# Dividing softmax weights before the transposes: sums, splits and a later place for decoding

## The chip, the cores and the metric

The kernel runs on one core of a Trainium2 chip. The metric is device time in microseconds (us), the median of several executions. The engines are named as in the profile: PE is TensorE (PEld its weight loads), DVE is VectorE, ACT is ScalarE, POOL is GpSimd, SP issues DMAs. SBUF is the on-chip memory, PSUM the accumulator memory that PE writes.

## The reference, cut to what matters

Attention over q, k, v of shape (8, 8, 576, 64) keeps for each query the 32 largest scores, takes a softmax over them and multiplies by v. The result, 4608 tokens of width 512, goes through a layer without nonlinearity but a product:

```python
scores = scale * np.matmul(q, k.transpose(0, 1, 3, 2))
kth = np.partition(scores, -top_k, axis=-1)[..., -top_k:-top_k + 1]
scores = np.where(scores >= kth, scores, -1000000000.0)
attn = np.exp(scores - np.max(scores, axis=-1, keepdims=True))
attn = attn / (np.sum(attn, axis=-1, keepdims=True) + 1e-09)
x = np.matmul(attn, v)          # heads side by side: 4608 x 512
out = ((x @ w1) * (x @ w2)) @ w3 @ w_out
```

## The kernel before

Attention is cut into 144 slots. A *wide* slot is 128 queries of two heads (128 of them), an *ends* slot is the last 64 queries of four heads (16, two in each of the 8 batches). Twelve slots make 384 tokens, a block, and each of the 12 blocks is one pass through the layer (`moe_steps`): 192 matmuls into tiles `ab`, whose two halves are multiplied (ACT copies one half into `asb`, DVE multiplies, ACT and POOL write the high and low parts `g`), then 96 matmuls into `eo`. The kernel multiplies every operand as a high part and a low part, three products each: `x` has both, and so have `wh`/`wl`, `wf` and `g`.

The order on each engine is the order of the code (`InOrder`). The loop over p is a pipeline: iteration p takes the scores of slot p+1 (`scores`, PE into `st`, `take_scores`, ACT into `s`), picks the largest 32 of slot p (`top32_steps`, DVE), masks and exponentiates slot p-1 (`mask`, ACT and POOL; `exps`, ACT with a sum into `sums`), and turns slot p-2 and multiplies it by v. In between stand three calls of `fill`, each of 8 matmuls of the layer (`SHARE`), which also issue what the last finished product put off (`evict`), and seven *places* for start-up work (`warm`): at a place, each unit of weights under way takes one step. A unit loads 512 KB (`fetch`), is decoded from 64-bit storage (`decode`: ACT into `t` and `z`, then DVE, then POOL) and used: `load_w12` splits it, `load_w3` folds it on PE into `pf` (w3 and w_out are multiplied into one weight, `wf`). Forty units fill the first dozen slots; a new one starts at every second place.

For slot m = p-2 the order is: `invert` (POOL adds 1e-9 to the sums, DVE takes reciprocals), `spread` (POOL copies a wide slot's two reciprocals over 128 columns, tile `wide`), `turn` (PE transposes the weights `pab` into `tp` and `ro`, and `wide` into a further part of `ro`), `take_turned` (ACT copies `tp` into `pts` and `ro` into `pr`), `values` (PE multiplies by v, into columns 256 to 384 of `ro`; for an ends slot it also spreads the reciprocals with 8 small matmuls, which ACT copies), `normalise` (DVE multiplies the product by the turned reciprocals, in place in `pr`), `split_high` (ACT writes the high part of x from `pr`) and, in the next iteration, `split_low` (POOL subtracts to get the low part). `ro` has one buffer, `tp` and `st` share two.

Of the kernel before, what the change touches and what calls it, by code (L numbers as in the profile page):

```python
# [68 lines left out]
def attn_moe(ctx: ExitStack, tc: tile.TileContext, q, k, v, w1, w2, w3, w_out, out, flag, general):  # L69
# [44 lines left out]
    def decode(z, dst=None):  # L114
        t = ps_e.tile([128, CHUNK], F32, tag="t", name="t")
        high = z[:, 1 : 2 * CHUNK : 2]
        low = z[:, : 2 * CHUNK].bitcast(U16)[:, 1 : 4 * CHUNK : 4]
        r, u = z[:, 0 : 2 * CHUNK : 2].bitcast(I32), z[:, 2 * CHUNK :].bitcast(I32)
        act.activation(t, high, AF.Copy, scale=2.0**-112)
        act.activation(r, low, AF.Copy, scale=2.0**-13)  # L120
        yield
        ti = t.bitcast(I32)
        dve.tensor_scalar(u, ti, -(2**31), None, op0=ALU.bitwise_and)
        dve.scalar_tensor_tensor(u, ti, 3, u, op0=ALU.logical_shift_left, op1=ALU.bitwise_or)
        yield
        dst = z[:, 2 * CHUNK :] if dst is None else dst
        pool.tensor_tensor(dst.bitcast(I32), u, r, op=ALU.add)
        yield
        yield
        return dst  # L130
# [137 lines left out]
        pool.tensor_scalar(sums, sums, 1e-9, None, op0=ALU.add)  # L268
        dve.reciprocal(sums, sums)

    def spread(sums, hps):
        if len(hps) == 2:
            return None
        wide = att_p.tile([128, 128], F32, tag="wide", name="wide", bufs=1)
        pool.tensor_copy(wide[:].rearrange("p (a d) -> p a d", a=2), sums[:].unsqueeze(2).to_broadcast([128, 2, D]))
        return wide

    def turn(pab, wide):
        tp = ps_a.tile([128, 2, 512], F32, tag="a", name="tp")
        flat = pab[:].rearrange("p a c -> p (a c)")  # L280
        for a in range(2):
            for c in range(4):
                o = a * (S + 64) + c * 128
                pe.transpose(tp[:, a, c * 128 : (c + 1) * 128], flat[:, o : o + 128], ident)
        ro = ps_v.tile([128, 512], F32, tag="v", name="ro")
        pe.transpose(ro[:, :128], flat[:, 512:640], ident)
        if wide is not None:
            pe.transpose(ro[:, 128:256], wide, ident)
        return tp, ro

    def take_turned(tp, ro, wide):
        pts = att_p.tile([128, 2, 512], F32, tag="pts", name="pts", bufs=1)
        act.copy(pts, tp)
        pr = att_p.tile([128, 256], F32, tag="pr", name="pr", bufs=1)
        n = 128 if wide is None else 256
        act.copy(pr[:, :n], ro[:, :n])
        return pts, pr[:, :128], pr[:, 128:]

    def values(vts, hps, pts, pr, rec, sums, ro):
        rb, ov = ro[:, 128:256], ro[:, 256:384]  # L300
        ends = len(hps) == 2
        for i, h in enumerate(HEADS):
            if ends:
                for j in range(2):
                    pe.matmul(
                        rb[h, j * 64 : j * 64 + 64], sums[:, j : j + 1].to_broadcast([128, 64]), ident[:, HEADS[i ^ j]],
                        start=True, stop=True,
                    )
        for j, hp in enumerate(hps):
            vt = vts[hp]  # L310
            for c in range(5):
                for i, h in enumerate(HEADS):
                    block = i * 4 + c if c < 4 else (((8, 10), (10, 9))[j][i] if ends else 8 + i)
                    n = HEADS[i ^ j] if ends else slice(0, 128)
                    rhs = pr[:, n] if c == 4 else pts[:, j if ends else i, c * 128 + n.start : c * 128 + n.stop]
                    to = ov[h, j * 64 : j * 64 + 64] if ends else ov[h]
                    pe.matmul(to, vt[:, block * D : (block + 1) * D], rhs, start=(c == 0), stop=(c == 4))
        if ends:
            act.copy(rec, rb)
        return ov  # L320

    def width(t):
# [1 line left out]

    def new_x(n):
        return x_p[n % 2].tile([128, 2, NB], F32R, tag="x", name="x")

    def normalise(ov, rec):
        dve.tensor_tensor(rec, ov, rec, op=ALU.mult)

    def parts_of(tiles, lo, t, whole):
        n = width(t)
        return [(x[:, 0, lo : lo + n], x[:, 1, lo : lo + n], whole[:, j * n : j * n + n]) for j, x in enumerate(tiles)]
# [2 lines left out]
        act.copy(high, whole)  # L336

    def split_low(high, low, whole):
        pool.tensor_tensor(low, whole, high.bitcast(F32), op=ALU.subtract)

    def moe_steps(xs, nb, places, after):
        def take_a(p, asb):
# [46 lines left out]
    if general:  # L389
        outs = out.rearrange("e (b t) -> b e t", b=B)  # L390
        for src, step in startup:
            for _ in step(fetch(src)):
                pass
        settle()
        with tc.For_i(0, B, 1) as b:
            seen = small.tile([1, 1], I32, tag="seen", name="seen", bufs=1)
            nc.sync.dma_start(seen, flag[ds(b + 1, 1), :])
            with tc.If(nc.values_load(seen, min_val=0, max_val=1) > 0):
                kts = {hp: load_k(b, hp) for hp in range(NHP)}
                vts = {hp: load_v(b, hp) for hp in range(NHP)}  # L400
                for first, ts in ((0, range(3)), (NB, range(3, TAIL + 1))):
                    xs, lo = [new_x(0) for _ in range(NHP)], 0
                    for t in ts:
                        qt = load_q(b, t)
                        for hps in [hps for hps, u in slots_of(0) if u == t]:
                            s, st = new_s(), scores(qt, kts, hps)
                            for h in range(2):
                                take_scores(s, st, h)
                            edge = top32_exact(s)
                            pab, sums = new_weights()  # L410
                            for a in range(2):
                                mask(s, edge, pab, a)
                                exps(edge, pab, sums, a)
                            invert(sums)
                            wide = spread(sums, hps)
                            tp, ro = turn(pab, wide)
                            pts, pr, rec = take_turned(tp, ro, wide)
                            ov = values(vts, hps, pts, pr, rec, sums, ro)
                            normalise(ov, rec)
                            for part in parts_of([xs[hp] for hp in hps], lo, t, rec):  # L420
                                split_high(*part)
                                split_low(*part)
                        lo += width(t)
                    place = lambda es: outs[ds(b, 1)][:, es, first : first + lo].rearrange("o p n -> (o p) n")
                    for _ in moe_steps(xs, lo, [(place, slice(0, lo))], lambda f: f()):
                        pass
        return
# [72 lines left out]
    def warm():  # L500
        entered.append(p)
        if p < 0:
            return
        if fetched and len(entered) % 2 == 0:
            z, step = fetched.pop(0)
            going.append(step(z))
        going[:] = [unit for unit in going if next(unit, "end") != "end"]
        prefetch(WAITING)
# [9 lines left out]
    for p in range(-1, n_slots + 3):  # L518
        i, j, m = p + 1, p - 1, p - 2
        finder = top32_steps(ss[p], p) if 0 <= p < n_slots else iter(())  # L520
        if 0 <= m < n_slots:
            invert(pabs[m][1])
        folded = next(finder, None)
        warm()
        if 0 <= j < n_slots:
            edges[j] = edges_of(j)
        for part in fresh:
            split_low(*part)
        fresh.clear()
        if 0 <= m < n_slots:  # L530
            wide = spread(pabs[m][1], slots[m][1])
        if 0 <= j < n_slots:
            pabs[j] = new_weights()
            for a in range(2):
# [3 lines left out]
        begin()  # L538
        next(finder, None)
        if 0 <= m < n_slots:  # L540
            tp, ro = turn(pabs[m][0], wide)
            pts, pr, rec = take_turned(tp, ro, wide)
        if 0 <= j < n_slots:
            exps(edges[j], *pabs[j], 0)
        warm()
# [14 lines left out]
                renew_q(group_of[i] + 2)  # L560
        if 0 <= m < n_slots:
            b, hps, t = slots[m]
            ov = values(of(vts, b), hps, pts, pr, rec, pabs[m][1], ro)
            renew(vts, load_v, m)
        next(finder, None)
        warm()
# [3 lines left out]
        if 0 <= m < n_slots:  # L570
            n = m // BLOCK
            for hp in hps:
                if (n, hp) not in xs:
                    xs[n, hp] = new_x(n)
            normalise(ov, rec)
            fresh += parts_of([xs[n, hp] for hp in hps], column[group_of[m]], t, rec)
            for part in fresh:
                split_high(*part)
            del ss[m], pabs[m], edges[m]
            if (m + 1) % BLOCK == 0:  # L580
                starting.append(n)
# [67 lines left out]
```

## Time and profile before

| what | value |
|---|---|
| time of three runs | 1297.02 us median, 1296.96 to 1297.53 |
| the profiled execution's own time | 1297.56 us |
| its span | 1295.8 us |
| busy PE / PEld / DVE / ACT / POOL | 1225.3 / 1044.9 / 1178.8 / 954.4 / 840.7 us |
| granted TensorE clock, mean over the span | 0.973 |

The profiled execution runs from its first instruction to its last in 1295.8 us; 1.8 us lie around that. Busy time is the time in which an engine has an instruction under way; a busy PE counts matmuls that overlap each other, so its weight loads (PEld) are shown beside it. The run has three stretches: the start-up with the decoding of weights, up to about 193 us; the steady slots, up to about 1225 us; and the last block, which PE does alone.

### The profile page before, as it was taken

How to read it: one execution, taken by the hardware profiler on the slowest of the kernel's cores; microseconds unless marked ns; L12 is line 12 of the kernel's file. 1: busy time of each engine (PE TensorE's matmuls, PEld its weight loads, DVE VectorE, ACT ScalarE, POOL GpSimd, SP SyncE). 2: the span in 40 equal slices, each digit the busy share in tenths (PEclk: the TensorE clock that was granted, in tenths of full speed). 3: DMA queues.
4: the chain of work that ended last, by engine and by line, in shares of the span. 5: the costliest groups of instructions: out<-in, count | busy, mean ns of one | idle time of the engine just before them, and what ended most of it. 6: DMA issues, size and time to landing. Idle time of an engine off the chain costs nothing.

```text
span 1295.8 us, 27725 instructions
## 1 busy us (share of the span) xinstructions
PE 1225.3 (95%) x9617; PEld 1044.9 (81%) x9617; DVE 1178.8 (91%) x3932; ACT 954.4 (74%) x1961; POOL 840.7 (65%) x1169
## 2 busy tenths in 40 slices
PE   3788769999999999999999999999999999999996
PEld 1444448888888888888888888888888888888996
DVE  7899999999999999999999999999999999999610
ACT  5677777777777778777777778777777778777621
POOL 4777887757757757657657666767667666667520
PEclk7799969999999999999999999999999999999999
DMA  7334402110220012100210012000210011000000
GB/s 279 106 122 131 128 19 76 37 34 9 61 67 9 10 34 81 38 28 19 65 53 10 16 48 83 16 28 20 68 50 10 22 62 63 22 22 2 19 8 28
DMA packets 30122, 64.79 MB, mean 50 GB/s; under 512 B 5396, under 2 KB 11540, under 8 KB 29972
## 3 DMA queue, kind: packets, MB, share of 16 engines
q1 hardware_dynamic: 29972, 62.93, 14.8%
q8 instruction: 77, 1.26, 0.4%
q14 instruction: 73, 0.60, 0.1%
HBM read 53.48 MB, written 9.44 MB: 49 GB/s over the span
## 4 chain that ended last, share of the span: by engine, by line
PE 89%; DVE 5%; ACT 3%; POOL 2%; issue 1%; DMA 0%; SPq 0%; POOLq 0%; DVEq 0%; ACTq 0%
PE ab L58 33%; PE eo L58 16%; PE ro L58 16%; PE st L58 12%; PE tp L58 9%; PE pf L58 3%; DVE w L58 2%; DVE z L58 2%; POOL z L58 1%; DVE top L58 1%; ACT pab L58 1%; ACT z L58 0%; ACT s L58 0%; POOL wl L58 0%; ACT t L58 0%
## 5 line engine op out<-in xcount | busy, mean ns | idle before, releaser
L58 POOL TENSOR_TENSOR pab<-s,pab 128x576 f32<-128x576 f32 x288 | 404.1, 1425 | 127.2 <-DVE w L58 109.8
L58 DVE MAX8 top<-w 128x8 f32<-128x192 f32 (+1 forms) x1152 | 467.1, 447 | 0.0
L58 PE MATMUL ab<-x,wh 128*128 128x384 f32 x1536 | 403.6, 344 | 0.0
L58 ACT COPY pts<-tp 128x1024 f32<-128x1024 f32 x144 | 146.1, 1015 | 196.7 <-PE tp L58 196.7
L58 DVE MATCH_REPLACE8 w<-top,w 128x192 f32<-128x192 f32 x864 | 289.2, 342 | 0.0
L58 PEld LDWEIGHTS ab<-x,wh 128*128 128x128 f32 x1536 | 275.3, 189 | 0.0
L58 PE MATMUL ab<-x,wl 128*128 128x384 f32 x768 | 269.5, 351 | 0.0
L58 ACT ACTIVATE pab<-pab,edge 128x576 f32<-128x576 f32 x288 | 226.8, 788 | 0.9 <-POOL pab L58 0.9
L58 PE MATMUL eo<-g,wf 128*128 128x384 f32 x1152 | 225.8, 346 | 0.0
L58 ACT ACTIVATE pab<-s,edge 128x576 f32<-128x576 f32 x288 | 207.5, 768 | 15.6 <-POOL edge L58 15.6
L58 PEld LDWEIGHTS eo<-g,wf 128*128 128x128 f32 x1152 | 198.6, 188 | 7.5 <-issue 7.5
L58 ACT COPY s<-st 128x576 f32<-128x576 f32 x288 | 184.5, 641 | 18.8 <-PE st L58 18.8
L58 PE MATMUL st<-kt,qt 64*128 64x288 f32 (+1 forms) x1280 | 186.4, 439 | 12.5 <-DMA kt<-in_k 7.7
L58 DVE TENSOR_TENSOR w<-w,s 128x384 f32<-128x384 f32 x288 | 183.4, 637 | 4.9
L58 DVE TENSOR_TENSOR w<-s 128x384 f32<-128x384 f32 x288 | 168.1, 624 | 8.1 <-ACT s L58 7.6
L58 PEld LDWEIGHTS ro<-pts,vt 128*64 128x64 f32 x2560 | 129.2, 138 | 50.6 <-ACT g L58 28.3
L58 PE MATMUL ro<-pts,vt 128*64 128x128 f32 (+1 forms) x2560 | 162.3, 270 | 0.0
L58 PE MATMUL tp<-ident,pab 128*128 128x128 f32 x1152 | 151.7, 275 | 11.1 <-POOL wo L58 9.7
L58 PEld LDWEIGHTS st<-kt,qt 64*128 64x128 f32 (+1 forms) x1280 | 99.6, 181 | 74.5 <-ACT pr L58 30.4
L58 PEld LDWEIGHTS ab<-x,wl 128*128 128x128 f32 x768 | 144.3, 188 | 13.4 <-issue 12.3
L58 PEld LDWEIGHTS tp<-ident,pab 128*128 128x128 f32 x1152 | 136.1, 142 | 21.3 <-POOL wo L58 10.2
L58 POOL TENSOR_TENSOR g<-asb,g 128x384 fp32r<-128x384 f32 x96 | 96.8, 1009 | 86.4 <-ACT g L58 86.4
(51 smaller groups left out, 1259.8 us busy)
## 6 DMA issues: line engine op xcount, KB each, us to landing
z<-in_w SPq DMA_DIRECT2D x32, 512.0 KB, 3.6
vt<-in_v SPq DMA_DIRECT2D x32, 352.0 KB, 3.4
qt<-in_q SPq DMA_DIRECT2D x40, 256.0 KB, 2.7
kt<-in_k SPq DMA_DIRECT2D x32, 320.0 KB, 3.0
out_t<-osb SPq DMA_DIRECT2D x32, 192.0 KB, 1.9
z<-in_wo SPq DMA_DIRECT2D x8, 512.0 KB, 6.4
out_t<-osb SPq DMA_DIRECT2D x16, 160.0 KB, 1.8
out_t<-osb SPq DMA_DIRECT2D x16, 32.0 KB, 1.6
```

Of the source, the lines that this page charges most:

```text
L58: ins = fn(*args, **kw)
```

## The change

The weights of a slot are divided by their sums on ACT before they are transposed: `normalise` now takes the reciprocals as a scale for each partition and rewrites both halves of `pab`, two instructions of 128x576. `spread`, the tile `wide`, its transpose, the 8 small matmuls of an ends slot and ACT's copy of them go. The product by v is then x itself: `split_high` reads it from the bank `ro`, and `split_low`, which also reads that bank, moves from POOL to DVE, ahead of a place. `decode` yields once more, so everything after a unit's decoding happens a place later.

```diff
@@ decode
         pool.tensor_tensor(dst.bitcast(I32), u, r, op=ALU.add)
+        yield
         yield
         yield
@@
-    def spread(sums, hps):
...
-    def turn(pab, wide):
+    def normalise(pab, rec):
+        for a in range(2):
+            act.activation(pab[:, a, :], pab[:, a, :], AF.Copy, scale=rec[:, a : a + 1])
+
+    def turn(pab):
...
-        if wide is not None:
-            pe.transpose(ro[:, 128:256], wide, ident)
...
-        pr = att_p.tile([128, 256], F32, tag="pr", name="pr", bufs=1)
-        n = 128 if wide is None else 256
-        act.copy(pr[:, :n], ro[:, :n])
+        pr = att_p.tile([128, 128], F32, tag="pr", name="pr", bufs=1)
+        act.copy(pr, ro[:, :128])
...
-        for i, h in enumerate(HEADS):
-            if ends:
-                for j in range(2):
-                    pe.matmul(
-                        rb[h, j * 64 : j * 64 + 64], sums[:, j : j + 1].to_broadcast([128, 64]), ident[:, HEADS[i ^ j]],
-                        start=True, stop=True,
-                    )
...
-        if ends:
-            act.copy(rec, rb)
...
-    def normalise(ov, rec):
-        dve.tensor_tensor(rec, ov, rec, op=ALU.mult)
...
-        pool.tensor_tensor(low, whole, high.bitcast(F32), op=ALU.subtract)
+        dve.tensor_tensor(low, whole, high.bitcast(F32), op=ALU.subtract)
@@ the loop over p
         folded = next(finder, None)
+        for part in fresh:
+            split_low(*part)
+        fresh.clear()
         warm()
         if 0 <= j < n_slots:
             edges[j] = edges_of(j)
-        for part in fresh:
-            split_low(*part)
-        fresh.clear()
         if 0 <= m < n_slots:
-            wide = spread(pabs[m][1], slots[m][1])
+            normalise(*pabs[m])
...
-            normalise(ov, rec)
-            fresh += parts_of([xs[n, hp] for hp in hps], column[group_of[m]], t, rec)
+            fresh += parts_of([xs[n, hp] for hp in hps], column[group_of[m]], t, ov)
```

ACT, one steady slot in which `ab` products are put away; `x` is the high part, `pab<-s,edge` the mask, `pab,sums<-pab,edge` the exponential. Before:

```order
L58 COPY s<-st 128x2x288
L58 CAST x<-pr 128x128
L58 ACTIVATE pab<-s,edge 128x576 x2
L58 COPY asb<-ab 128x384
L58 COPY pts<-tp 128x1024
L58 COPY pr<-ro 128x256
L58 ACTIVATE pab,sums<-pab,edge 128x576
```

and after:

```order
L58 COPY s<-st 128x2x288
L58 CAST x<-ro 128x128
L58 ACTIVATE pab<-pab,sums 128x576 x2
L58 ACTIVATE pab<-s,edge 128x576 x2
L58 COPY asb<-ab 128x384
L58 COPY pts<-tp 128x1024
L58 COPY pr<-ro 128x128
L58 ACTIVATE pab,sums<-pab,edge 128x576
```

The two divisions stand between x and the next slot's masks, ahead of `asb` and `pts`; the copy into `pr` is half as wide.

DVE, from the last search of one slot into the next. Before:

```order
L58 MAX top_96<-w 128x8 x2
L58 TENSOR_TENSOR pr<-ro,pr 128x128
L58 RECIPROCAL sums<-sums 128x2
L58 TENSOR_TENSOR w<-s 128x2x192 x2
L58 TENSOR_TENSOR w<-w,s 128x2x192 x2
L58 MAX top_97<-w 128x8 x2
```

and after:

```order
L58 MAX top_96<-w 128x8 x2
L58 RECIPROCAL sums<-sums 128x2
L58 TENSOR_TENSOR w<-s 128x2x192 x2
L58 TENSOR_TENSOR w<-w,s 128x2x192 x2
L58 TENSOR_TENSOR x<-ro,x 128x128
L58 MAX top_97<-w 128x8 x2
```

The multiplication ahead of the reciprocal is gone, and the subtraction stands behind the four folding steps.

PE in the start-up, from the product by v to the next slot's; `pf` is the fold of w3. Before:

```order
L58 MATMUL ro<-pr,vt 64x128 x2
L58 MATMUL pf_953<-wo,z 128x512 x6
L58 MATMUL tp<-ident,pab 128x128 x8
L58 MATMUL ro<-ident,pab 128x128
L58 MATMUL ro<-ident,wide 128x128
L58 MATMUL pf_1062<-wo,z 128x512 x2
L58 MATMUL st<-kt,qt 128x288 x4
```

and after:

```order
L58 MATMUL ro<-pr,vt 64x128 x2
L58 MATMUL pf_1077<-wo,z 128x512 x8
L58 MATMUL tp<-ident,pab 128x128 x8
L58 MATMUL ro<-ident,pab 128x128
L58 MATMUL st<-kt,qt 128x288 x4
```

The two fold matmuls between the transposes and the scores now stand with the six behind the product by v.

## Rows read from the trace of the kernel before

**Rows 1.** The page: the chain that ended last, by engine.

```profile
PE 89%; DVE 5%; ACT 3%; POOL 2%; issue 1%; DMA 0%; SPq 0%; POOLq 0%; DVEq 0%; ACTq 0%
```

**Rows 2.** Stretches: length, busy us of each engine (instructions), clock, DMA share, GB/s.

```profile
core 0: us, PE busy (x) PEld busy (x) DVE busy (x) ACT busy (x) POOL busy (x), PEclk, DMA share, GB/s
28.59:192.68 164.09, 124.89 (x623) 69.72 (x624) 150.10 (x416) 122.58 (x234) 126.92 (x143) 0.84 0.32 102
...
431.39:439.29 7.90, 7.90 (x64) 6.97 (x63) 7.87 (x28) 6.30 (x13) 6.07 (x9) 1.00 0.00 0
455.16:463.10 7.94, 7.94 (x64) 7.00 (x63) 7.56 (x28) 5.91 (x12) 4.40 (x8) 1.00 0.08 27
```

**Rows 3.** The chain in order of time, one steady slot: start, us, work.

```profile
446.90 3.02 PE eo L58 x16
449.92 0.87 PE tp L58 x8
450.80 0.22 PE ro L58 x2
451.02 1.41 PE eo L58 x8
452.42 1.17 PE st L58 x8
453.59 1.24 PE ro L58 x20
```

**Rows 4.** Timeline of PE's loads, one steady slot; idle before and releaser bracketed.

```profile
460.29 0.79 PEld L58 LDWEIGHTS st<-kt,qt 64*128 64x128 f32 x8 [0.25 <-ACT pr L58]
461.46 0.85 PEld L58 LDWEIGHTS ro<-pts,vt 128*64 128x64 f32 x16 [0.38 <-ACT osb L58]
...
462.70 1.36 PEld L58 LDWEIGHTS eo<-g,wf 128*128 128x128 f32 x8 [0.17 <-issue]
```

**Rows 5.** The same in an ends slot, where the sums are spread.

```profile
516.93 0.32 PEld L58 LDWEIGHTS ro<-ident,sums 128*64 128x64 f32 x8 [0.39 <-ACT g L58]
517.16 0.56 PEld L58 LDWEIGHTS ro<-pts,vt 128*64 128x64 f32 x16
```

**Rows 6.** Timeline of ACT, the slot from 431.39 us.

```profile
431.71 1.44 ACT L58 ACTIVATE pab<-s,edge 128x576 f32<-128x576 f32 x2
433.06 0.46 ACT L58 COPY asb<-ab 128x384 f32<-128x384 f32 x1
434.97 1.01 ACT L58 COPY pts<-tp 128x1024 f32<-128x1024 f32 x1 [1.46 <-PE tp L58]
435.88 0.38 ACT L58 COPY pr<-ro 128x256 f32<-128x256 f32 x1
```

**Rows 7.** Timeline of DVE and POOL, the same slot.

```profile
431.46 1.00 DVE L58 TENSOR_TENSOR w<-s 128x384 f32<-128x384 f32 x2
432.01 0.78 POOL L58 TENSOR_TENSOR x<-pr,x 128x128 fp32r<-128x128 f32 x1
432.38 1.41 DVE L58 TENSOR_TENSOR w<-w,s 128x384 f32<-128x384 f32 x2
433.71 0.61 DVE L58 MAX8 top<-w 128x8 f32<-128x192 f32 x2
433.94 2.81 POOL L58 TENSOR_TENSOR pab<-s,pab 128x576 f32<-128x576 f32 x2 [0.59 <-DVE w L58]
434.89 0.55 DVE L58 TENSOR_TENSOR asb<-ab,asb 128x384 f32<-128x384 f32 x1
...
439.09 0.29 DVE L58 TENSOR_TENSOR pr<-ro,pr 128x128 f32<-128x128 f32 x1
439.29 0.15 DVE L58 RECIPROCAL sums<-sums 128x2 f32<-128x2 f32 x1
```

**Rows 8.** The chain in order of time, a slot of the start-up.

```profile
104.83 5.36 PE pf L58 x12
...
110.21 0.59 ACT wf L58
```

More of the change, by code (lines that the diff above doesn't have):

```diff
@@ L269, in invert @@
         dve.reciprocal(sums, sums)
-    def spread(sums, hps):
[L272 to L276, printed above, removed]
-    def turn(pab, wide):
+    def normalise(pab, rec):
+        for a in range(2):
+            act.activation(pab[:, a, :], pab[:, a, :], AF.Copy, scale=rec[:, a : a + 1])
+    def turn(pab):
         tp = ps_a.tile([128, 2, 512], F32, tag="a", name="tp")
@@ L286, in turn, with take_turned, values @@
         pe.transpose(ro[:, :128], flat[:, 512:640], ident)
-        if wide is not None:
-            pe.transpose(ro[:, 128:256], wide, ident)
         return tp, ro
-    def take_turned(tp, ro, wide):
+    def take_turned(tp, ro):
         pts = att_p.tile([128, 2, 512], F32, tag="pts", name="pts", bufs=1)
         act.copy(pts, tp)
-        pr = att_p.tile([128, 256], F32, tag="pr", name="pr", bufs=1)
-        n = 128 if wide is None else 256
-        act.copy(pr[:, :n], ro[:, :n])
-        return pts, pr[:, :128], pr[:, 128:]
-    def values(vts, hps, pts, pr, rec, sums, ro):
-        rb, ov = ro[:, 128:256], ro[:, 256:384]
-        ends = len(hps) == 2
-        for i, h in enumerate(HEADS):
-            if ends:
-                for j in range(2):
-                    pe.matmul(
-                        rb[h, j * 64 : j * 64 + 64], sums[:, j : j + 1].to_broadcast([128, 64]), ident[:, HEADS[i ^ j]],
-                        start=True, stop=True,
-                    )
+        pr = att_p.tile([128, 128], F32, tag="pr", name="pr", bufs=1)
+        act.copy(pr, ro[:, :128])
+        return pts, pr
+    def values(vts, hps, pts, pr, ro):
+        ov = ro[:, 256:384]
+        ends = len(hps) == 2
         for j, hp in enumerate(hps):
@@ L414, in attn_moe @@
                             invert(sums)
[L415 to L418, printed above, removed]
-                            normalise(ov, rec)
-                            for part in parts_of([xs[hp] for hp in hps], lo, t, rec):
+                            normalise(pab, sums)
+                            tp, ro = turn(pab)
+                            pts, pr = take_turned(tp, ro)
+                            ov = values(vts, hps, pts, pr, ro)
+                            for part in parts_of([xs[hp] for hp in hps], lo, t, ov):
                                 split_high(*part)
@@ L540, in attn_moe @@
         if 0 <= m < n_slots:
-            tp, ro = turn(pabs[m][0], wide)
-            pts, pr, rec = take_turned(tp, ro, wide)
+            tp, ro = turn(pabs[m][0])
+            pts, pr = take_turned(tp, ro)
         if 0 <= j < n_slots:
@@ L562, in attn_moe @@
             b, hps, t = slots[m]
-            ov = values(of(vts, b), hps, pts, pr, rec, pabs[m][1], ro)
+            ov = values(of(vts, b), hps, pts, pr, ro)
             renew(vts, load_v, m)
@@ L574, in attn_moe @@
                     xs[n, hp] = new_x(n)
-            normalise(ov, rec)
-            fresh += parts_of([xs[n, hp] for hp in hps], column[group_of[m]], t, rec)
+            fresh += parts_of([xs[n, hp] for hp in hps], column[group_of[m]], t, ov)
             for part in fresh:
```

## The prediction

> **What bounds the kernel now.** I read the chain that ended last first, then the stretches, then single slots. The chain is PE for 89% of the span [rows 1]. In order of time a steady slot is a closed row of PE work: 3.02 us (16 matmuls of the layer), 0.87 (eight transposes), 0.22 (two more, the second that of `wide`), 1.41 (8 matmuls), 1.17 (scores), 1.24 (product by v), in all 7.93 us [rows 3]. Two slots side by side say the same: one that puts `ab` products away has DVE busy 7.87 of 7.90 us, one in the `eo` part has DVE busy 7.56 of 7.94, and both take as long [rows 2]. An engine that set the time could not do 0.31 us less in the second without the slot getting shorter, so DVE, though nearly full, is not what the steady slots wait for. PE is. In a slot of the `ab` part ACT is busy 6.30 us and stands idle 1.46 in one piece ahead of `pts`, for the transposes [rows 2, 6].
>
> PE's loads leave 0.25 + 0.38 + 0.17 us between them in such a slot [rows 4]. The profile names ACT for two of these gaps and nothing for the third, but an ends slot has 0.39 us at the same place [rows 5], with other work on ACT; I read them as the price of going to another shape of matmul and back, and leave them in the sum.
>
> The start-up is another matter. From 28.59 to 192.68 us 13 slots take 164.1 us, 12.6 each, with DVE busy 150.1 us of it and PE 124.9 [rows 2]. Its chain goes through PE's folds, 5.36 us in one piece, and on to ACT's copy of the folded weight [rows 8]. The last stretch is PE alone on the last block; the change leaves it as it is.
>
> **The change part by part.** Steady slots first, PE. A wide slot loses the transpose of `wide`: two transposes take 0.22 us of the chain, so one is 0.11 [rows 3]. An ends slot loses 8 loads and matmuls that take 517.16 - 516.93 = 0.23 us from start to start [rows 5]; the gap of 0.39 in front of them stays, for the product by v follows. About 131 slots have their PE part behind 193 us, 16 of them ends slots: 115 x 0.11 + 16 x 0.23 = 12.7 + 3.7 = 16.3 us, all of it on the chain, if no other engine steps in. The new slot is 7.82 us.
>
> ACT. Two divisions of 128x576 from SBUF to SBUF with one operand for each partition are added. The trace has no such copy; the nearest row is the mask, an instruction of the same shape with one such operand, two of which take 433.06 - 431.71 = 1.35 us from start to start [rows 6]. Low end: 0, if ACT's idle time hides it all (less than that it cannot be, for instructions are added and none goes that is as long); high end: 1.8 to 2.0, twice the pace of the 128x1024 copy (435.88 - 434.97 = 0.91) or its duration of 1.01 [rows 6]. I take 1.35, since the shape is the same. The copy into `pr` halves from 256 columns; against `asb` (384 columns, 0.46 us; 256 take 0.38) 128 columns are worth some 0.1 us [rows 6], an estimate. `split_high` costs what it did. So an `ab` slot has 6.30 + 1.35 - 0.1 = 7.55 us of ACT in 7.82, an `eo` slot 5.91 + 1.25 = 7.16. What hides it is the idle 1.46 us ahead of `pts`; of that 1.46 - 1.25 - 0.11 = 0.1 is left, and a little more where x waited for DVE. Behind the divisions in ACT's queue stand the masks, `asb` and `pts`: if the cover is gone, `pts` is late, then the product by v, and each 0.1 us costs 131 x 0.1 = 13 us.
>
> The divisions wait for DVE's reciprocal, which no longer stands behind the multiplication; the transposes come 16 layer matmuls (3.02 us) behind the product by v, and the divisions need 1.35 of that plus x, so PE should not wait for them.
>
> DVE. It loses the multiplication (0.20 us, 439.29 - 439.09) and gets the subtraction, of the same shape and with one operand in PSUM as well: 0.20, or 0.29 at its full duration [rows 7]. The first pair of folding steps takes 432.38 - 431.46 = 0.92 us and the second 433.71 - 432.38 = 1.33 while POOL reads SBUF for x [rows 7]. POOL's x and `wide` go, so the second pair should come down to 0.92: 0.41 saved, 7.87 to 7.46. POOL only gains; its next mask waits for the folding [rows 7], which ends earlier. None of this is on the chain of the steady slots; it is worth nothing there. `ro` has one buffer and is now held until the subtraction, but PE writes it again only behind 16 layer matmuls and the transposes, some 3.9 us after the product; folding and subtraction need 1.84 + 0.2 from the reciprocal on.
>
> Start-up. DVE saves the same 0.41 us in 13 slots, 5.3 us, and here DVE is the fullest. It is idle 164.1 - 150.1 = 14.0 us. The later place takes away part of that: eight fold matmuls now stand in one piece behind the product by v, with their input decoded a place earlier, and ACT's copy of the folded weight no longer stands ahead of `pts`. At best all 14.0 go, 19.3 in all; at worst none of it, and ACT's 13 x 1.25 = 16.3 us fall on the chain instead: +16.3 - 5.3 = 11 us lost. ACT is busy 122.6 of 164.1 and goes to 139, still below DVE's 145. I take half of the idle time: 7.0 + 5.3 = 12.3 us.
>
> The sum: 1297.56 - 16.3 - 12.3 = 1269 us against the profiled execution, which lies 0.5 us above the median of the runs, within what they differ.
>
> **The rivals.** First, *ACT and DVE close a loop.* `asb` now stands behind the divisions, and DVE's product of the halves waits for it. From that product to the next reciprocal DVE takes 439.29 - 434.89 - 0.20 = 4.20 us [rows 7]; then come the reciprocal (0.08 from start to start), divisions 1.35, masks 1.35, `asb` 0.46 [rows 6], and two hand-overs of 0.15, as from DVE's folding (432.38 + 1.41 = 433.79) to POOL's mask at 433.94 [rows 7]: 7.74 us. That is below 7.82 by 0.08, so it is no luxury. If it comes out at 7.9 or more, the 86 slots of the `ab` part keep their old length and the gain is that of the `eo` and ends slots (some 8 us) and 4 to 9 us of the start-up: 1281 to 1286, up to 1291 if the start-up gives nothing.
>
> Second, the slow side: *the divided copy costs what the 1024-wide one does*, 0.91 to 1.01 us each. It decides from the point where the pair exceeds 7.93 - 6.20 = 1.73 us in an `ab` slot. At 1.82 to 2.02, ACT needs 8.02 to 8.22; 86 slots lose up to 0.29 us, 25 us, the `eo` slots (5.91 - 0.1 + 2.02 = 7.83) still gain 4, and the start-up gives about nothing: 1305 to 1318. For it speaks only that no such copy stands in the trace; against it the mask's row.
>
> Third, *nothing to be measured*: the start-up's chain does run through ACT in places [rows 8], and 13 x 1.35 = 17.5 us there would cancel the 16.3 of PE: about 1299.
>
> Fourth, *PE has room.* If the gaps of [rows 4] are waits for ACT that go, PE needs only 7.00 - 0.11 = 6.89 us and ACT and DVE set the slots: 7.55 in 8 of 12, 7.16 in 4, on average 7.42, so 131 x 0.51 = 67 us and the start-up's 12.3 go: 1218. The equal gaps in slots with different ACT work speak against it. The Trainium skill (Perfetto Trace Analysis, section Identifying the Most-Contended Engine) says to judge PE by the busy share of its weight loads and not by that of its matmuls. By that rule PE is at 88% here, 7.00 of 7.94, DVE would be the most contended engine, and this fourth case would be the one; the trace does not agree, for the slot keeps its 7.94 us where DVE has 0.38 idle.
>
> **How the numbers follow.** Forecast 0.62, the loop 0.18, slow copies 0.10, nothing 0.07, room on PE 0.03. The predicted time is the forecast's, 1269. Its own range is 1262 (start-up at its best) to 1281 (the start-up gives nothing). The range reaches over the loop to 1291 and down to 1260, and leaves out 0.20. What three runs can tell from no change is about 0.2%, 2.6 us. Faster: 0.62 + 0.18 + 0.03 = 0.83; same: 0.07; slower: 0.10.
>
> **What would show it.** Right: the steady slot on the chain is 7.8 us, all PE, with 0.11 for the one transpose into `ro`; the two divisions start 0.68 us apart; both pairs of folding steps take 0.92 us; DVE has 0.3 us idle in every slot; a start-up slot takes about 11.7 us. The loop: DVE's product of the halves waits for `asb`, and `ab` slots are longer than `eo` slots. Wrong: PE's transposes or its product by v wait for ACT, the gaps of [rows 4] change, or the start-up is longer than 164 us.

## The result, and the profile after

The changed kernel takes 1273.7 us, the median of four runs (1272.59 to 1274.07), against 1296.99 for the kernel before on the same chip: a ratio of 0.982, 95% interval 0.980 to 0.984. The prediction was 1269, range 1260 to 1291. The span of the profiled execution went from 1295.8 to 1272.2 us, its own time from 1297.56 to 1274.04. By stretches, cut at DVE's reciprocals as in [rows 2]:

| stretch | before, us | after, us | difference | predicted |
|---|---|---|---|---|
| up to the first reciprocal | 28.59 | 28.50 | -0.1 | 0 |
| start-up, 13 slots | 164.09 | 156.53 | -7.6 | -12.3 |
| steady slots, the next 130 | 1032.06 | 1015.55 | -16.5 | -16.3 |
| the rest of the span | 71.1 | 71.6 | +0.5 | 0 |

So the steady slots gave what was forecast, to 0.2 us, and the start-up gave 4.7 us less. The chain by engine, which answers [rows 1]:

```profile
PE 86%; ACT 7%; POOL 2%; DVE 2%; issue 1%; DMA 0%; SPq 0%; POOLq 0%; DVEq 0%
```

ACT, which had 3% of it, now has 7; how much of that is real is asked below, with the start-up. These are the stretches after: the start-up, one start-up slot, an `ab` slot, an `eo` slot, all steady slots. The columns are those of [rows 2].

```profile
28.50:185.03 156.53, 119.29 (x618) 69.05 (x619) 143.43 (x416) 136.22 (x260) 111.58 (x116) 0.89 0.34 107
113.81:126.04 12.23, 10.77 (x54) 5.67 (x54) 11.66 (x34) 11.01 (x21) 8.73 (x9) 1.00 0.39 130
419.82:427.65 7.83, 7.83 (x62) 6.90 (x63) 7.73 (x29) 7.39 (x16) 4.71 (x6) 1.00 0.01 2
451.07:458.89 7.82, 7.82 (x62) 6.89 (x63) 7.29 (x26) 6.98 (x15) 3.37 (x5) 1.00 0.08 27
185.03:1200.58 1015.55, 1015.55 (x8366) 894.67 (x8367) 979.25 (x3460) 942.11 (x1922) 557.60 (x738) 1.00 0.12 37
```

An `ab` slot and an `eo` slot still take the same 7.82 us, though DVE is busy 7.73 us in one and 7.29 in the other, and ACT 7.39 and 6.98. The part of the chain in order of time that changed answers [rows 3]; behind it stand PE's loads of the same slot, which answer [rows 4].

```profile
447.09 0.11 PE ro L58
```

```profile
448.53 0.79 PEld L58 LDWEIGHTS st<-kt,qt 64*128 64x128 f32 x8 [0.24 <-issue]
449.70 0.85 PEld L58 LDWEIGHTS ro<-pts,vt 128*64 128x64 f32 x16 [0.39 <-ACT osb L58]
```

The row of two transposes at 0.22 us has become one at 0.11; everything else on PE is as before, the gaps too (0.24 and 0.39 against 0.25 and 0.38; the third is 0.17 in both).

ACT and DVE in an `ab` slot, for [rows 6] and [rows 7]:

```profile
427.88 1.47 ACT L58 ACTIVATE pab<-pab,sums 128x576 f32<-128x576 f32 x2
429.22 1.45 ACT L58 ACTIVATE pab<-s,edge 128x576 f32<-128x576 f32 x2
...
431.48 1.02 ACT L58 COPY pts<-tp 128x1024 f32<-128x1024 f32 x1 [0.44 <-PE tp L58]
```

```profile
427.88 1.03 DVE L58 TENSOR_TENSOR w<-s 128x384 f32<-128x384 f32 x2
428.82 1.14 DVE L58 TENSOR_TENSOR w<-w,s 128x384 f32<-128x384 f32 x2
429.88 0.28 DVE L58 TENSOR_TENSOR x<-ro,x 128x128 fp32r<-128x128 f32 x1
```

The two divisions take 1.34 us from start to start, 0.67 each, and the idle time ahead of `pts` went from 1.46 to 0.44 us. The second folding pair went from 1.33 to 429.88 - 428.82 = 1.06 us, not to 0.92.

The start-up is where the surprise is. Six of its slots, from 64.89 to 138.28 us, are alike, 12.23 us each. This is how DVE ends one of them, and POOL beside it:

```profile
111.36 0.69 DVE L58 SCALAR_TENSOR_TENSOR z<-t,z 128x512 int32<-128x512 int32 x1
...
113.81 0.17 DVE L58 RECIPROCAL sums<-sums 128x2 f32<-128x2 f32 x1 [0.43 <-POOL sums L58]
```

```profile
112.19 1.29 POOL L58 TENSOR_TENSOR z<-z 128x512 int32<-128x512 int32 x1 [1.00 <-ACT t L58]
113.56 0.21 POOL L58 TENSOR_SCALAR sums<-sums 128x2 f32<-128x2 f32 x1
```

DVE finishes its last decoding step of the slot at 111.36 + 0.69 = 112.05 us. POOL's decoding addition (`z`, 1.29 us), which adds what that step made, starts 0.14 us later; the addition of 1e-9 to the sums stands behind it in POOL's queue; and DVE's reciprocal waits for the sums, 0.43 us in idle time. That is a ring: DVE from the reciprocal at 101.58 us to its last decoding step, POOL's two additions, DVE again, 12.23 us in all. PE's folds, which [rows 8] showed on the chain, are not in it.

The profile names another releaser for POOL's addition, ACT's `t`, which ends at 112.18 us, and so its chain of this slot runs through ACT, and ACT's share rises. But that `t` belongs to a later unit of weights, and the addition doesn't read it. In the kernel before with the later place alone (run further down) there is no such coincidence, and the delay is the same:

```profile
111.18 0.69 DVE L58 SCALAR_TENSOR_TENSOR z<-t,z 128x512 int32<-128x512 int32 x1
...
113.12 0.27 DVE L58 TENSOR_TENSOR pr<-ro,pr 128x128 f32<-128x128 f32 x1
113.62 0.17 DVE L58 RECIPROCAL sums<-sums 128x2 f32<-128x2 f32 x1 [0.23 <-POOL sums L58]
```

```profile
112.01 1.29 POOL L58 TENSOR_TENSOR z<-z 128x512 int32<-128x512 int32 x1 [1.06 <-ACT s L58]
```

DVE's step ends at 111.18 + 0.69 = 111.87 us and POOL starts 0.14 us later, while the copy `s` that is named had ended 0.8 us before. Two runs that give ACT more work settle it; they stand under "How much room ACT has".

### The profile page after: what moved, and what is told of

Same layout as the page of the kernel before. It is cut to its first block, busy times and chain, and to the rows that moved or that the text cites. A ratio compares the mean times of both kernels' runs of the same rounds, so it can differ in the third digit from the quotient of the medians.

```text
span 1272.2 us, 27178 instructions
## 1 busy us (share of the span) xinstructions
PE 1201.4 (94%) x9361; PEld 1026.4 (81%) x9361; DVE 1149.0 (90%) x3948; ACT 1106.6 (87%) x2233; POOL 688.7 (54%) x881
## 4 chain that ended last, share of the span: by engine, by line
PE 86%; ACT 7%; POOL 2%; DVE 2%; issue 1%; DMA 0%; SPq 0%; POOLq 0%; DVEq 0%
PE ab L58 33%; PE eo L58 17%; PE ro L58 14%; PE st L58 12%; PE tp L58 9%; ACT pab L58 3%; POOL z L58 1%; ACT t L58 1%; ACT z L58 1%; DVE w L58 1%; ACT s L58 1%; PE pf L58 1%; DVE z L58 1%; POOL wl L58 0%; DVE top L58 0%
## 5 line engine op out<-in xcount | busy, mean ns | idle before, releaser
L58 ACT ACTIVATE pab<-pab,sums 128x576 f32<-128x576 f32 x288 | 211.5, 796 | 19.2 <-DVE sums L58 19.2
L58 DVE TENSOR_TENSOR w<-w,s 128x384 f32<-128x384 f32 x288 | 159.3, 553 | 4.9
L58 DVE TENSOR_TENSOR w<-s 128x384 f32<-128x384 f32 x288 | 148.8, 557 | 16.0 <-ACT s L58 7.5
L58 PEld LDWEIGHTS st<-kt,qt 64*128 64x128 f32 (+1 forms) x1280 | 98.4, 180 | 71.6 <-issue 34.3
```

Of the source, the lines that this page charges most:

```text
L58: ins = fn(*args, **kw)
```

## The experiments

**PE's part put back.**

```diff
+        if len(hps) == 1:
+            pe.transpose(ro[:, 128:256], flat[:, :128], ident)
@@ values
+        for i, h in enumerate(HEADS):
+            if ends:
+                for j in range(2):
+                    pe.matmul(
+                        rb[h, j * 64 : j * 64 + 64], sums[:, j : j + 1].to_broadcast([128, 64]), ident[:, HEADS[i ^ j]],
+                        start=True, stop=True,
+                    )
```

> The changed kernel with PE's removed work put back as dead work: for a wide slot one more transpose of 128x128 into columns 128 to 256 of ro (its input is a part of pab, nobody reads it), for an ends slot the 8 small matmuls. ACT, DVE and POOL stay as changed. If PE sets the steady slots: slots go back from 7.82 to 7.93 us (ends from 7.90 to 8.14), some 16 us more, 1290. If ACT or DVE set them, or the gain came from the DVE and POOL work that went: 1274 to 1277. I expect 1290.

Measured: 1290.04 us, ratio to the kernel before 0.994 (0.993 to 0.996), 16.3 us above the changed kernel. The steady slots, and one `ab` slot:

```profile
184.47:1216.68 1032.21, 1032.21 (x8608) 910.89 (x8609) 982.33 (x3461) 953.67 (x1922) 542.68 (x738) 1.00 0.12 37
423.15:431.08 7.93, 7.93 (x63) 7.00 (x64) 7.75 (x28) 7.46 (x16) 4.39 (x6) 1.00 0.00 0
```

1032.21 us is what the kernel before needs (1032.06), although DVE and POOL keep all they gained: DVE has 7.75 us of work in 7.93. PE's transposes, with the small matmuls of the ends slots, make the difference alone.

**PE's part alone.** The copy into `pr` keeps its 256 columns by reading 128 of them twice, and in an ends slot `rec` is copied from those columns too. The reciprocals are left out, so the output is not the reference's.

```diff
-        if wide is not None:
-            pe.transpose(ro[:, 128:256], wide, ident)
...
-        act.copy(pr[:, :n], ro[:, :n])
+        if wide is None:
+            act.copy(pr[:, :128], ro[:, :128])
+        else:
+            act.copy(pr[:].rearrange("p (a d) -> p a d", a=2), ro[:, :128].unsqueeze(1).to_broadcast([128, 2, 128]))
...
-                    pe.matmul(
-                        rb[h, j * 64 : j * 64 + 64], sums[:, j : j + 1].to_broadcast([128, 64]), ident[:, HEADS[i ^ j]],
-                        start=True, stop=True,
-                    )
```

> The kernel before without PE's part alone: no transpose of wide and no small matmuls in ends slots; the copy of 256 columns reads the first 128 of ro twice, so the product is multiplied by weights and not by reciprocals (output not the reference's). If PE alone sets the steady slots: 7.93 to 7.82 us, 16 us less, 1281, the start-up as before (164 us). If DVE at 7.87 us of busy time is a bound as well: slots of the ab part stay at 7.87 to 7.93 and only the eo and ends slots gain, 6 to 8 us, 1289 to 1291. I expect 1281 to 1285, since DVE at 7.87 us stands above the new slot of 7.82 in 8 of 12 slots.

Measured: 1279.71 us, ratio 0.986 (0.985 to 0.988), 17.6 us less than before.

```profile
192.18:1207.62 1015.44, 1015.44 (x8365) 894.56 (x8364) 996.58 (x3445) 803.30 (x1677) 709.53 (x998) 1.00 0.12 37
403.70:411.53 7.83, 7.83 (x63) 6.90 (x62) 7.79 (x28) 6.30 (x13) 6.02 (x9) 1.00 0.09 32
```

The steady slots need 1015.44 us, the changed kernel's 1015.55. So the divisions on ACT and the subtraction on DVE neither help nor hurt there. DVE fits into 7.83 us without any of its savings; the expectation's doubt on that falls.

**The later place, undone and alone.** Taken out of the changed kernel:

```diff
         pool.tensor_tensor(dst.bitcast(I32), u, r, op=ALU.add)
-        yield
         yield
         yield
```

> The changed kernel without the further yield in decode: fold, split and copy of a unit of weights go a place earlier, as before. The steady slots do not see it. The prediction had the later place take part of DVE's idle time in the start-up: then 3 to 7 us slower, 1277 to 1281. Rival: the start-up slot of 12.2 us is set by ACT's chain through the reciprocal, which waits for POOL's addition to the sums behind a decoding addition that stands at the same place in both: then within 1.5 us of 1274.

And put into the kernel before, as its only change:

```diff
         pool.tensor_tensor(dst.bitcast(I32), u, r, op=ALU.add)
+        yield
         yield
         yield
```

> The kernel before with the further yield in decode alone. Steady slots unchanged at 7.93 us. By the prediction's reason the start-up gets 3 to 7 us shorter than 164 us: 1290 to 1294. Rival: the yield does nothing by itself, 1295.5 to 1298.5, and the start-up's 7.6 us came from the folding steps, DVE's and POOL's work that went.

Measured: 1276.27 us (0.984; 0.982 to 0.985) without it, 2.6 us above the changed kernel, with intervals that overlap. That is in neither band of its expectation (1277 to 1281, or up to 1275.5). Its profiled execution, the longest of the four (1278.82), has a start-up of 160.7 us, 4.2 more, and the same steady slots. In the kernel before, the later place alone gives 1289.94 us (0.994; 0.993 to 0.996), 7.3 less. The start-up and one slot of it, kernel before with the later place:

```profile
28.60:184.70 156.10, 121.79 (x623) 69.00 (x624) 146.63 (x416) 122.04 (x234) 127.38 (x143) 0.85 0.34 107
113.62:125.91 12.29, 10.88 (x56) 5.79 (x55) 11.91 (x33) 9.90 (x20) 10.02 (x11) 1.00 0.40 129
```

Without it, in the changed kernel, the slots in the middle of the start-up are uneven, 12.2 to 14.1 us. The longest, and ACT in it:

```profile
79.41:93.53 14.12, 12.85 (x62) 6.70 (x59) 11.85 (x33) 12.37 (x24) 8.68 (x9) 1.00 0.43 130
```

```profile
85.01 0.59 ACT L58 CAST wf<-pf 128x512 fp32r<-128x512 f32 x1 [1.27 <-PE pf L58]
```

There 12 fold matmuls stand in one piece ahead of the transposes and ACT waits 1.27 us for the last of them, with `pts` queued behind. With the later place six slots in the middle are alike, 12.23 us in the changed kernel and 12.28 to 12.29 in the kernel before. So the rival of the second expectation falls: in the kernel before the later place is worth 8.0 us of start-up, which is the whole gain of the change there (156.10 against 156.53).

**The addition to the sums taken out of the ring.**

```diff
     def invert(sums):
-        pool.tensor_scalar(sums, sums, 1e-9, None, op0=ALU.add)
         dve.reciprocal(sums, sums)
+
+    def add_small(sums):
+        pool.tensor_scalar(sums, sums, 1e-9, None, op0=ALU.add)
@@ the end of an iteration, ahead of its last place
+        if 0 <= j < n_slots:
+            add_small(pabs[j][1])
         warm()
```

> The changed kernel with POOL's addition of 1e-9 to the sums issued an iteration earlier, ahead of the last place, right after the exponentials, so that it no longer stands behind a decoding addition; at the start of the next iteration only DVE's reciprocal is left. If the start-up slot of 12.23 us is set by the chain decoding addition, sums, reciprocal, divisions: DVE's wait of 0.43 us goes and the slot comes down to 11.7 to 11.8, its next bound being DVE at 11.66 us busy; slots 9 to 11 of the start-up gain up to 1 us each: 1267 to 1271. Rival, that ACT's or DVE's decoding work is what is late: the start-up stays at 156 us, 1273 to 1275. Steady slots: no change by either, 7.82 us.

Measured: 1268.91 us, ratio 0.978 (0.977 to 0.980), 4.8 us below the changed kernel. The start-up, one slot of it, and the shares of the chain from 76 to 101 us:

```profile
27.96:179.50 151.54, 122.69 (x618) 70.76 (x619) 146.91 (x416) 137.09 (x260) 113.54 (x117) 0.83 0.35 111
110.26:122.09 11.83, 10.77 (x55) 5.68 (x54) 11.65 (x34) 11.13 (x21) 8.74 (x10) 1.00 0.40 132
```

```profile
by line: DVE z L58 33.6%; DVE w L58 27.8%; DVE top L58 23.0%; issue 9.0%; DVE wf L58 4.8%; DVE x L58 3.4%; DVE sums L58 0.6%
```

The ring is open: DVE no longer waits for POOL ahead of the reciprocal, and the chain is DVE's, as the prediction had assumed of the changed kernel: 11.83 us a slot where it said 11.7. The start-up comes down by 5.0 us to 151.5, where the prediction had put it (164.1 - 12.3 = 151.8); the steady slots stay at 1015.56, so the addition cost nothing there. This version is the fastest of all that ran.

**The same on the kernel before,** with the later place as well (both edits above).

> The kernel before with the further yield and with the addition to the sums issued early, so that the chain decoding addition, sums, reciprocal is gone here too. What is left between it and the changed kernel with the early addition (1268.9) is then the change's division, its DVE work and PE's transposes. If DVE's shorter folding steps pay as soon as DVE is the start-up's bound: a start-up slot is 0.25 us longer than that kernel's 11.84, 12.05 to 12.1, the start-up some 155 us and the time 1286 to 1289, 3 us of it the folding steps. If the folding steps are hidden there too: 11.8 to 11.9 us a slot, 1284 to 1286.

Measured: 1287.37 us (0.992; 0.990 to 0.993). The start-up, a slot of it, and one that stands out:

```profile
27.98:182.42 154.44, 123.44 (x623) 70.00 (x624) 148.84 (x417) 122.16 (x234) 129.09 (x144) 0.88 0.36 109
112.14:124.07 11.93, 10.88 (x55) 5.79 (x54) 11.79 (x34) 9.91 (x19) 10.06 (x12) 1.00 0.47 134
50.94:64.52 13.58, 13.05 (x60) 6.74 (x59) 11.89 (x35) 9.92 (x19) 9.85 (x11) 1.00 0.34 110
```

The time lies in the band of the first theory, the slot (11.93) near that of the second. A slot is 0.10 us longer than with the change, not 0.25; of the 2.9 us between the two start-ups, 1.3 come from the slot of 13.58 us (12.24 with the change), in which PE is the busiest with 13.05. From the first folding step to what follows the second pair DVE takes 112.47 - 110.44 = 2.03 us with the change and 114.46 - 112.21 = 2.25 without, 0.22 less; but from the reciprocal to the first folding step it takes 110.44 - 110.26 = 0.18 us with the change and 112.21 - 112.14 = 0.07 without. So 0.11 is left of the 0.22. Why the folding starts later there stays open.

**How much room ACT has.** A copy of 128x256 that nobody reads, and then a third copy of 128x576 in place, both behind the divisions:

```diff
             normalise(*pabs[m])
+            junk = att_p.tile([128, 256], F32, tag="junk", name="junk", bufs=1)
+            act.copy(junk, pabs[m][0][:, 0, :256])
```

```diff
             normalise(*pabs[m])
+            act.activation(pabs[m][0][:, 1, :], pabs[m][0][:, 1, :], AF.Copy, scale=1.0)
```

> The changed kernel with one more copy on ACT in each slot, 128x256 from SBUF to a tile that nobody reads, behind the divisions; an estimate from the rows of other copies is 0.25 to 0.3 us. ACT goes to 7.65 us busy in ab slots, below 7.82. If only PE's 7.82 us and each engine's own busy time count: steady slots stay, the start-up gains up to 13 x 0.3, 1274 to 1278. By the first rival of the prediction the loop reciprocal, divisions, masks, asb, DVE's product, searches, reciprocal stands at 7.7 us: with 0.28 more it is 7.9 to 8.0, the 88 ab slots get 0.1 to 0.2 longer and DVE's product waits for asb, 1285 to 1295, the eo slots unchanged.

> The changed kernel with a third copy of 128x576 in place behind the two divisions (factor 1, so the output stays): the three take 2.0 us, which is what the prediction's slow side put on the pair (1.82 to 2.02). That rival's sum, 1305 to 1318, took only ACT's busy time, 7.38 + 0.67 = 8.05 us, against the slot. If the loop through asb sets the ab slots instead, it is 7.7 + 0.67 = 8.4 us, 88 x 0.55 = 48 us more, with 9 in the start-up about 1330. If ACT had room for it: 1274 to 1283.

Measured: 1274.34 us with the small one (0.982; 0.981 to 0.984), which can't be told from the changed kernel; an `ab` slot and its ACT:

```profile
419.65:427.48 7.83, 7.83 (x62) 6.90 (x62) 7.74 (x29) 7.70 (x17) 5.08 (x6) 1.00 0.01 3
```

```profile
435.48 1.45 ACT L58 ACTIVATE pab<-pab,sums 128x576 f32<-128x576 f32 x2
...
437.13 1.44 ACT L58 ACTIVATE pab<-s,edge 128x576 f32<-128x576 f32 x2
```

With the large one it is 1304.19 us (1.005; 1.003 to 1.007), 30.5 above the changed kernel. An `ab` slot, DVE's product and ACT's masks behind it, and the chain in order of time from there to the next product:

```profile
430.60:438.82 8.22, 8.05 (x63) 6.78 (x62) 7.73 (x28) 8.06 (x17) 5.06 (x6) 1.00 0.01 3
```

```profile
434.67 0.56 DVE L58 TENSOR_TENSOR asb<-ab,asb 128x384 f32<-128x384 f32 x1 [0.42 <-ACT asb L58]
...
441.07 1.43 ACT L58 ACTIVATE pab<-s,edge 128x576 f32<-128x576 f32 x2
```

```profile
439.01 1.46 ACT pab L58 x2
...
442.50 0.37 ACT asb L58
...
442.90 0.56 DVE asb L58
```

This is the loop of the prediction's first rival, closed: 442.90 - 434.67 = 8.23 us, longer than ACT's 8.06 busy. The masks begin 441.07 - 439.01 = 2.06 us behind the divisions, 0.72 more than the 1.34 of the changed kernel, so without the third copy the loop comes to 8.23 - 0.72 = 7.51 us, not 7.74. The small copy puts the masks 437.13 - 435.48 = 1.65 us behind the divisions, 0.31 more: 7.82, just what PE leaves it. The `eo` slots, which have no `asb`, come out at 7.5 to 7.8 us, as DVE catches up with PE, and give part of it back; 130 steady slots take 1043.99 us, 28.4 more, not the 48 that the loop's expectation charged for the `ab` slots alone. The price that the prediction put on its slow side was near (1305 to 1318), by another mechanism than it named.

The same two runs tell whether ACT is in the ring of the start-up. A slot of it with the small copy and one with the large one, and what ACT and POOL do at the end of the first:

```profile
101.21:113.44 12.23, 10.77 (x54) 5.68 (x54) 11.66 (x34) 11.30 (x22) 8.73 (x9) 1.00 0.43 131
103.18:115.41 12.23, 10.77 (x54) 5.68 (x54) 11.66 (x34) 11.65 (x22) 8.72 (x9) 1.00 0.39 129
```

```profile
111.43 0.67 ACT L58 ACTIVATE t<-z 128x512 f32<-128x512 f32 x1
...
111.81 1.29 POOL L58 TENSOR_TENSOR z<-z 128x512 int32<-128x512 int32 x1 [0.68 <-ACT x L58]
```

ACT has 0.3 and 0.6 us more to do in the slot, and the slot is 12.23 us as before; POOL's addition starts in the middle of ACT's `t`, so it doesn't wait for it. ACT is not in the ring. Three later slots, of 13.30, 12.95 and 11.68 us in the changed kernel, do grow with the small copy, by 0.3 us each; what sets them was not worked out.

**What POOL's reading costs DVE.**

```diff
+        if late and p < n_slots:
+            idle = att_p.tile([128, 128], F32, tag="idle", name="idle", bufs=1)
+            pool.tensor_tensor(idle, ident, ident, op=ALU.subtract)
         if 0 <= m < n_slots:
             normalise(*pabs[m])
```

> The changed kernel with a subtraction of 128x128 in SBUF put back on POOL where the low part of x was made before, from constants into a tile that nobody reads, in steady slots alone. It tells what POOL's reading costs DVE: if it is what made the second pair of folding steps 1.33 us, the pair goes from 1.14 back to 1.33 or more, and the four steps from 2.22 to 2.46 us. DVE then has 7.85 to 7.96 us in ab slots. If DVE is the second bound, they get 0.03 to 0.14 us longer, 1277 to 1286. If PE alone sets them (prediction: DVE's saving is worth nothing in the steady slots): 1273 to 1275. If the folding steps do not slow down, POOL's reading was not the cause.

Measured: 1275.33 us (0.983; 0.981 to 0.985), 1.6 above the changed kernel, which these intervals can't tell apart, and just outside the band of "PE alone". POOL's subtraction, DVE's second pair and what follows it, then an `ab` slot and a whole block of twelve slots:

```profile
428.89 0.71 POOL L58 TENSOR_TENSOR idle<-ident 128x128 f32<-128x128 f32 x1
...
429.27 1.34 DVE L58 TENSOR_TENSOR w<-w,s 128x384 f32<-128x384 f32 x2
430.53 0.28 DVE L58 TENSOR_TENSOR x<-ro,x 128x128 fp32r<-128x128 f32 x1
```

```profile
420.17:428.11 7.94, 7.94 (x64) 7.01 (x63) 7.87 (x29) 7.38 (x15) 5.38 (x7) 1.00 0.01 3
560.71:654.67 93.96, 93.96 (x733) 82.62 (x734) 92.68 (x320) 87.70 (x177) 59.65 (x80) 1.00 0.16 47
```

The pair takes 430.53 - 429.27 = 1.26 us from start to start instead of 1.06: the reading is the cause. `ab` slots, counted at DVE's reciprocal, are 0.12 us longer, which would be 10.6 us for 88 of them. But DVE catches up with PE in the `eo` slots (7.48, 7.47 and 7.66 us, then 7.82), and the block above takes 93.96 us against 93.84 in the changed kernel. What has to fit under PE's 7.82 us is therefore the mean over a block's twelve slots, not the fullest slot. The 130 slots take 1018.17 us, 2.6 more: ten blocks of 0.12 to 0.24 us make 1.7, and the last 0.9 is the lag that DVE has not yet made good where the count ends.

## Why the prediction was right, and where it was off

**PE sets the steady slots: right.** 16.3 us were forecast; 16.5 came, 16.3 went again with the transposes put back, and the kernel before got the same steady slots with PE's part alone. A whole ends slot came from 8.14 to 7.90 us, by about the 0.23 read from [rows 5]. The third rival did not come: ACT's divisions put no 17 us on the start-up, whose alike slots stay at 12.23 us even with more work on ACT. The fourth, that PE has room, is out: with ACT and DVE still below 7.8 us the slot followed PE's 0.11 both ways. PE's loads are busy 6.9 of 7.82 us, the rest being mostly the three gaps, which did not move when ACT's and DVE's work around them did. The Trainium skill (Perfetto Trace Analysis, section Identifying the Most-Contended Engine) judges PE by the busy share of its loads, beside its share of the peak arithmetic; by that share DVE would come before PE here, and the runs don't agree.

**The divisions: right.** 0.68 us each was forecast from the mask's row, 0.67 came; ACT is busy 7.39 and 6.98 us instead of 7.55 and 7.16, and 0.44 us of its idle time ahead of `pts` is left where 0.1 was forecast. The second rival's price did not come, and the run that put it in by hand (1304) shows that this was the term to watch. The low end of its sum, 1305, leaves out the 4 us that it lets the `eo` slots gain; with them it is 1301.

**The loop through `asb`: a right mechanism, 0.23 us too long.** It was summed to 7.74 and comes to 7.51. Most of it is that full durations and a hand-over of 0.15 us were added where the next instruction follows sooner: from the masks' start to DVE's product the sum had 1.35 + 0.46 + 0.15 = 1.96 us, the trace has 442.90 - 441.07 = 1.83. The cover is 0.31 us, not 0.08.

**The folding steps: a term mis-sized.** 0.41 us was to go from the second pair, down to 0.92 like the first. It went to 1.06, by 0.27, and POOL's reading accounts for 0.20 of that when it is put back. The two pairs were never alike: the second takes 1.06 us with nothing under way on POOL. POOL's copy into `wide` was not needed for the 1.33: in the ends slot from 502.64 us of the kernel before, which has no `wide`, the pair takes 504.96 - 503.64 = 1.32 us as well. DVE therefore has 0.10 us idle in an `ab` slot, not 0.3.

**The start-up: the step that failed.** The prediction compared busy times, ACT's 139 us with DVE's 145, let DVE be the bound, gave it 5.3 us for the folding and 7.0 for half its idle time. By the runs:

| kernel | start-up, us | DVE busy | DVE idle |
|---|---|---|---|
| before | 164.1 | 150.1 | 14.0 |
| before, later place | 156.1 | 146.6 | 9.5 |
| changed | 156.5 | 143.4 | 13.1 |
| changed, sums early | 151.5 | 146.9 | 4.6 |

The later place alone is worth 8.0 us, near the 7.0 that were put on it, but half of an idle time was a choice and not a sum, so that is luck: 4.5 us of it were idle time and 3.5 busy time, which the prediction did not count on.

The folding is what failed. The rest of the change takes 3.2 us of busy time from DVE (13 x 0.25), and all of it turns up as idle time. The ring says why. It counts DVE's work from the reciprocal to the last decoding step, and nothing behind that. The four folding steps are in it and got 0.27 us shorter. The multiplication that went had stood behind the last decoding step, at 113.12 us in the rows above, where DVE would have waited for POOL anyway; the subtraction that came, 0.20 us, stands ahead of it. So 0.07 is left of the 0.27: DVE needs 10.47 us from the reciprocal to the end of that step instead of 10.54, the slot came from 12.28 to 12.23, and DVE's wait grew from 0.23 to 0.43 us. The prediction set the two against each other at 0.20 each, as if it did not matter where in the slot they stand, and let DVE be the bound by its busy time alone. Its text looks at what stands ahead of the reciprocal on DVE; it does not go one step further, to POOL's addition and what stands ahead of that. With the addition out of the ring the start-up came to 151.5 us, where the prediction had it.

## What to carry to other kernels

When an engine waits in every slot for a small result of another engine, follow that result back through every queue that it passes, in each stage apart: here a 0.2 us addition behind a 1.3 us one cost 4.8 us, and issuing it a place earlier gave them back. In such a ring, work ahead of what the engine hands over counts in full and work behind it is hidden in the wait, so ask of moved work on which side it lands. The releaser that a trace names is an inference; adding work to that engine tells whether it is one. Where slots differ, ask of the second engine, and of a loop through several, whether its mean over a block fits under the first's. An engine that is nearly full is no bound by that: DVE at 7.79 of 7.83 us cost nothing.

## What the runs showed of the hardware

DVE and POOL slow each other in both directions when both read SBUF. POOL in a steady slot of the changed kernel, where DVE's first folding pair starts at 427.88 us:

```profile
427.81 0.20 POOL L58 TENSOR_TENSOR edge<-top,coef 128x4 f32<-128x4 f32 x1 [0.19 <-DVE sums L58]
427.95 0.54 POOL L58 TENSOR_TENSOR over<-top 128x2 f32<-128x2 f32 x1
```

`over` has half the elements of `edge` and takes 0.54 us against 0.20; the one starts just behind DVE's first step, the other just ahead of it. In an `eo` slot, where the folding starts at 443.48 us, `over` is ahead of it too and takes as little:

```profile
443.44 0.20 POOL L58 TENSOR_TENSOR over<-top 128x2 f32<-128x2 f32 x1
```

The other way round, the 0.71 us of a POOL subtraction made DVE's second pair 0.20 us longer, and in the start-up without the later place a longer instruction of POOL doubles the first pair, 2.12 us instead of 1.04:

```profile
155.43 2.12 DVE L58 TENSOR_TENSOR w<-s 128x384 f32<-128x384 f32 x2
```

```profile
155.39 1.27 POOL L58 TENSOR_TENSOR wl<-z,wh 128x512 fp32r<-128x512 f32 x1
```

The three sizes fit together. The subtraction reached 428.89 + 0.71 - 429.27 = 0.33 us into DVE's pair, which lost 0.20; x in [rows 7] reached 432.01 + 0.78 - 432.38 = 0.41 us into it, which lost 1.33 - 1.06 = 0.27; `wl` reached 155.39 + 1.27 - 155.43 = 1.23 us into it, which lost 2.12 - 1.04 = 1.08. Each time the loss is the overlap less some 0.14 us. The Trainium skill (SBUF — State Buffer, section Who interferes with whom) says that a DVE instruction with two inputs in SBUF and a GpSimd instruction that reads SBUF exclude each other, the later one waiting for the earlier to end. These rows agree, but for the 0.14 us.
